# Attention ahead of a mixture of experts: values masked on TensorE, copied by ScalarE, contiguous loads, a later comparison on GpSimd

## The chip, the cores and the metric

The kernel runs on one core of a Trainium2 chip. The metric is the device time of one execution in microseconds (us), as the median of several runs. The profile shows one execution: TensorE appears as PE (matmuls) and PEld (weight loads), VectorE as DVE, ScalarE as ACT, GpSimd as POOL, SyncE as SP, whose queue issues most transfers.

## The reference

```python
def _attn_ref(q, k, v):                    # B, H, S, D = 8, 8, 576, 64
    k_p = k.reshape(B, H, Sp, 8, D).mean(axis=3)      # Sp = 72
    v_p = v.reshape(B, H, Sp, 8, D).mean(axis=3)
    scores = np.matmul(q, k_p.transpose(0, 1, 3, 2)) / np.sqrt(D)
    scores = scores - np.max(scores, axis=-1, keepdims=True)
    attn = np.exp(scores)
    attn = attn / (np.sum(attn, axis=-1, keepdims=True) + 1e-09)
    return np.matmul(attn, v_p)
def reference(...):
    x = attention transposed to (4608, 512)
    x = _moe_ref(x, ...)   # logits = x @ w_gate; greedy choice in order of the logits,
                           # 576 tokens for each of 8 experts; relu(x @ w1[e]) @ w2[e]
    return _moe2_ref(x, ...)   # h = x @ w_in; (h - tanh(h)) @ w_out
```

## The kernel before, in words

The program has three stages: attention over 36 tiles of 128 tokens, the routing and the eight experts, and a dense layer. Each token tile j runs through `scores(j)` and `values(j)`. `scores` multiplies the queries `qT` with the pooled keys `kb` into PSUM (`sc`); VectorE takes the maximum (`mx`) and the difference (`dif`), ScalarE the exponential (`e`). `values` transposes `e` on TensorE (`pt`), ScalarE copies it to SBUF (`et`), TensorE multiplies it with the pooled values (`va`) into the one PSUM tile `av`, and VectorE divides by the sums (`r`, `t`, `x`) and writes the routing logits. A batch element is 576 tokens, so 4.5 tiles: tiles 4, 13, 22 and 31 hold tokens of two batch elements and are multiplied in halves. The last tile writes its product to `sc` instead of `av`.

`pool(b)` sums each eight keys and values of a batch element. For the first element VectorE does it, later GpSimd with six kinds of additions (`pf`, `pg`, then `kb` or `vb`). `rows_of_values(b)` then turns the values: TensorE multiplies `vb` with `turn`, which holds an identity and the gate weights, into 72 columns for each of three row groups; ScalarE copies them to `rows`; VectorE multiplies `rows` with one of two masks in `own` (which of the 96 rows belong to the first head and which to the second) and so fills both halves of `va`.

`first_best(js)` is called after tiles 17, 28, 33 and 35. It makes 32-bit keys of the largest logits: VectorE finds the largest (`m`, `oh`, `mw`, `ohb`), splits the key into `key`, casts it to `hl`, and, for the first two groups, GpSimd compares it with 127 thresholds (`at`, a subtraction and then a comparison with zero).

All of attention is recorded as operations with an urgency, and a planner (`Plan.emit`) writes them into each engine's queue by costs that it estimates. An engine then runs its queue in order. Nearly all instructions have line 123, the recorder's. After attention, routing, experts and the dense layer follow, placed by a plan of their own.

Of the kernel before, what the change touches and what calls it, by code (L numbers as in the profile page):

```python
# [9 lines left out]
F32 = mybir.dt.float32  # L10
# [5 lines left out]
AF = mybir.ActivationFunctionType  # L16
OP = mybir.AluOpType
AX = mybir.AxisListType

B, H, S, D = 8, 8, 576, 64  # L20
SP = S // 8
NP = H // 2
DM = H * D
N = B * S
NT = N // 128
E = 8
# [13 lines left out]

PA, PB1, PD1 = 0.0791790355214496, 0.051241577318574885, 0.039687888533833315
PB2, PD2 = -2.3308446993087815, 2.4448524213730685


class Ring:
# [225 lines left out]
class Kernel:  # L271
# [88 lines left out]
    def attention(self):  # L360
        nc, tc, io, c = self.nc, self.tc, self.io, self.c
        self.L = self.cp.tile([128, NT, 8], F32, name="logits")
        with ExitStack() as st:
            a1 = st.enter_context(tc.tile_pool(name="att1", bufs=1))
            ap = Ring(st.enter_context(tc.tile_pool(name="att", bufs=1)))
            ps = Ring(st.enter_context(tc.tile_pool(name="attp", bufs=1, space=bass.MemoryType.PSUM)), banks=True)
# [7 lines left out]
            half = [slice(0, 64), slice(64, 128)]  # L374


            wg = a1.tile([128, NP, 8], F32, name="wg")
            kb = [a1.tile([128, NP, 2 * SP], F32, name=f"kb{i}") for i in range(2)]
            vb = [a1.tile([128, 2, 3, 96], F32, name=f"vb{i}") for i in range(2)]
            va = [a1.tile([96, 2, 3, 2, 73], F32, name=f"va{i}") for i in range(2)]  # L380
            turn = a1.tile([128, 2, 3, 72], F32, name="turn")
            own = a1.tile([96, 3, 2], F32, name="own")
            junk = a1.tile([128, 512], BF, name="junk")
            nc.vector.memset(junk, 0.0)
            for x in (kb[0], vb[0], kb[1], vb[1]):
                nc.gpsimd.memset(x, 0.0)
            P = self.plan = Plan(nc)
            P.urgency = 900.0
# [1 line left out]

            def turns():
                P.urgency = -2.0
                for h in range(3):
                    for w, r0, r1, hh, pr, _ in parts[h]:
                        eye = c["ident"][half[hh], half[hh]]
                        P.scalar.activation(turn[half[hh], :, h, :64],
                                            eye[:, None, :].to_broadcast([64, 2, 64]), AF.Copy)
                        P.scalar.activation(turn[half[hh], :, h, 64:], wg[half[hh], pr::2], AF.Copy)
                        edge, op = (r1, OP.is_lt) if w == 0 else (r0, OP.is_ge)
                        P.vector.tensor_scalar(own[:, h, w:w + 1], c["pcol"][:96], float(edge), None, op0=op)  # L400
                        for i in range(2):
                            P.vector.tensor_scalar(va[i][:, :, h, w, 72], c["pcol"][:96].to_broadcast([96, 2]),
                                                   float(edge), 8.0, op0=op, op1=OP.mult)

            qT, raw = {}, {}

            def load(b):
                P.urgency = 4.5 * b - 12
                q = qT[b] = ap.tile([128, NP, S], F32, name="qT", bufs=3)
                kr = ap.tile([128, NP, SP, 8], F32, name="kr", bufs=2)  # L410
                vr = ap.tile([128, NP, SP, 8], F32, name="vr", bufs=2)
                raw[b] = kr, vr
                if b == 0:
                    for p in range(NP):
                        P.sync.dma_start(kr[:, p], io["k"][b, :, p])
                    for p in range(NP):
                        P.sync.dma_start(q[:, p, :128], io["q"][b, :, p, :128])
                    for hh in range(2):
                        P.sync.dma_start(wg[half[hh]], io["wg"].rearrange("(p h d) e -> h d p e", h=2, d=64)[hh])
                    for p in range(NP):  # L420
                        P.sync.dma_start(vr[:, p], io["v"][b, :, p])
                    for s0, s1 in ((128, 256), (256, S)):
                        for p in range(NP):
                            P.sync.dma_start(q[:, p, s0:s1], io["q"][b, :, p, s0:s1])
                else:
                    P.sync.dma_start(kr, io["k"][b])
                    P.sync.dma_start(q, io["q"][b])
                    P.sync.dma_start(vr, io["v"][b])
# [39 lines left out]
            def rows_of_values(b):  # L468
                P.urgency = 4.5 * b - 1.3
                for g in range(2):  # L470
                    pt = ps.tile([96, 3, 72], F32, name="pt", bufs=2)
                    for h in range(3):
                        P.tensor.matmul(pt[:, h], vb[b % 2][:, g, h], turn[:, g, h], start=True, stop=True)

                    rows = ap.tile([96, 3, 72], F32, name="rows", bufs=2)
                    P.scalar.activation(rows, pt, AF.Copy)
                    for w in range(2):
                        P.vector.tensor_tensor(va[b % 2][:, g, :, w, :72], rows,
                                               own[:, :, w:w + 1].to_broadcast([96, 3, 72]), op=OP.mult)

            tiles = []
            for j in range(NT):
                pieces, s = [], j * 128
                while s < (j + 1) * 128:
                    b = s // S
                    n = min((b + 1) * S, (j + 1) * 128) - s
# [4 lines left out]
            def scores(j):  # L491

                sc = ps.tile([128, 2, 512], F32, name="sc", bufs=2)
                for pr in range(NP):
                    for b, s0, p0, n in tiles[j]:
                        P.tensor.matmul(sc[p0:p0 + n, pr // 2, (pr % 2) * 144:(pr % 2) * 144 + 144],
                                        qT[b][:, pr, s0:s0 + n], kb[b % 2][:, pr, :], start=True, stop=True)
                sc = sc[:, :, 0:288].rearrange("p a (h s) -> p a h s", h=4)
                mx = ap.tile([128, 2, 4], F32, name="mx", bufs=2)
                P.vector.tensor_reduce(mx, sc, axis=AX.X, op=OP.max)  # L500
                dif = ap.tile([128, 2, 4, SP], F32, name="dif", bufs=2)
                P.vector.tensor_tensor(dif, sc, mx[:, :, :, None].to_broadcast([128, 2, 4, SP]), op=OP.subtract)
                e = ap.tile([128, 6 * 96], F32, name="e", bufs=2)
                P.scalar.activation(e, dif.rearrange("p a h s -> p (a h s)"), AF.Exp, scale=1.0 / 64)
                return e
# [38 lines left out]
            for name, shape, n in (("x", [128, 2, 4, 64], XB), ("t8", [128, 2, 4, 8], 2), ("et", [96, 2, 3, 128], 2),  # L544
                                   ("e", [128, 6 * 96], 2), ("r8", [128, 2, 4], 2)):
                ap.tile(shape, F32, name, n)
            load(0)
            pool(0)
            turns()
            load(1)  # L550
            E1 = {}
            for j in range(NT):
# [73 lines left out]
    def first_best(self, js, pool, engine):  # L626


        c, P = self.c, self.plan
        V = P.vector  # L630
        sg, key = self.best(js, True)
        self.hl = self.rp.tile([128, 2, NT], F32, name="hl")
        self.at7 = pool.tile([128, NT, 127], BF, name="at7")
        at, n = self.at7[:, js], js.stop - js.start
        x = key[:, 0, :, None].to_broadcast([128, n, 127])
        y = c["th7"][:, None, :].to_broadcast([128, n, 127])
        if engine == "vector":
            V.tensor_tensor(at, x, y, op=OP.is_ge)
        else:
            V.tensor_copy(self.hl[:, 0, js], key[:, 0])  # L640
            x = self.hl[:, 0, js, None].to_broadcast([128, n, 127])
            P.gpsimd.tensor_tensor(at, x, y, op=OP.subtract)
            P.gpsimd.tensor_scalar(at, at, 0.0, None, op0=OP.is_ge)
        V.tensor_scalar(sg, sg, 7, -(1 << 31), op0=OP.logical_shift_left, op1=OP.bitwise_xor)
        V.tensor_scalar(key[:, 1], sg, 7, None, op0=OP.arith_shift_right)
        if engine == "vector":
            V.tensor_copy(self.hl[:, :, js], key)
        else:
            V.tensor_copy(self.hl[:, 1, js], key[:, 1])

    def count(self, out, at, js, whole=False):

# [469 lines left out]
    half = [slice(q * HF, (q + 1) * HF) for q in range(2)]  # L1122
# [324 lines left out]
```

## Time and profile before

| what | value |
|---|---|
| time, median of 3 runs | 1525.25 us (1524.16 to 1530.08) |
| the profiled execution, its own time | 1525.06 us |
| its span | 1523.3 us |
| busy in the span: PE, PEld | 95%, 84% |
| busy in the span: DVE, ACT, POOL | 80%, 52%, 20% |
| attention, by the last tile's product | to about 166.7 us |

A share of the span is a mean over stages. Attention is the first ninth of the span; in it no one engine is busy throughout, and the granted clock of TensorE falls in places. The later stages are TensorE work from end to end.

### The profile page before, as it was taken

The page shows a single profiled execution, that of the slowest core. Times are in us where ns is not written, and L with a number is a line of the kernel's source. Part 1 is how long each engine was busy: PE and PEld are TensorE (multiplying, and loading weights), DVE is VectorE, ACT ScalarE, POOL GpSimd, SP SyncE. Part 2 cuts the span into 40 slices and gives each one's busy share as a digit, 9 for nine tenths or more (in the row PEclk, how much of TensorE's full clock was granted, in tenths as well). Part 3 has the DMA queues.
Part 4 walks back from the last instruction along what each step waited for, and adds up shares of the span by engine and source line. Part 5 has one row for each costly group of instructions (what it writes and reads, how often), then busy time and mean ns, then how long its engine had stood idle before and what let it go on. Part 6 is the DMA issues. An engine that isn't in the chain of part 4 may idle for free.

```text
span 1523.3 us, 25631 instructions
## 1 busy us (share of the span) xinstructions
PE 1450.4 (95%) x9764; PEld 1274.2 (84%) x9764; DVE 1218.8 (80%) x2548; ACT 795.7 (52%) x1435; POOL 309.6 (20%) x291
## 2 busy tenths in 40 slices
PE   8989687999999998999999999999999999999997
PEld 6878567999998998999878888888888888888885
DVE  8888777867898888876898788787878788787874
ACT  5334123233554536775666565655656565655653
POOL 4865021101132334553421000010100001010101
PEclk9989788999999999999999999999999999999999
DMA  9951123333342536775201010000101000000000
GB/s 346 352 194 63 43 88 90 101 110 122 128 140 98 168 129 195 261 246 188 93 28 56 1 35 22 28 29 1 56 1 42 14 29 28 23 33 1 28 1 28
DMA packets 100011, 138.51 MB, mean 91 GB/s; under 512 B 7472, under 2 KB 72496, under 8 KB 97200
## 3 DMA queue, kind: packets, MB, share of 16 engines
q1 hardware_dynamic: 89328, 108.04, 21.3%
q0 software_dynamic: 5952, 19.40, 3.7%
q10 hardware_dynamic: 4608, 9.44, 1.6%
q8 instruction: 76, 1.25, 0.3%
q14 instruction: 47, 0.39, 0.1%
HBM read 103.30 MB, written 33.55 MB: 90 GB/s over the span
## 4 chain that ended last, share of the span: by engine, by line
PE 48%; DVE 3%; DMA 1%; issue 1%; ACT 1%; POOL 0%; POOLq 0%; ACTq 0%; SPq 0%; DVEq 0%
PE mm L123 24%; PE m L123 12%; PE rt L123 6%; PE tr L123 6%; DVE g L123 2%; DVE gl L123 1%; DMA wr<-wd 1%; DMA yr<-yd 0%; DVE m L123 0%; ACT parts L123 0%; POOL out L1305 0%; ACT y L123 0%; DVE yl L123 0%; ACT t L123 0%; ACT u L123 0%
## 5 line engine op out<-in xcount | busy, mean ns | idle before, releaser
L123 PE MATMUL mm<-parts 128*128 128x288 f32 x2112 | 308.6, 301 | 3.8 <-DVE parts L123 3.8
L123 PEld LDWEIGHTS mm<-parts 128*128 128x128 f32 x2112 | 289.5, 190 | 7.1 <-DVE parts L123 3.9
L123 PE MATMUL mm<-parts,gh 128*128 128x512 f32 x792 | 244.0, 389 | 0.0
L123 DVE SCALAR_TENSOR_TENSOR g<-s,g 128x512 f32<-128x512 f32 x288 | 205.8, 715 | 2.8
L123 ACT ACTIVATE s<-u,pb 128x512 f32<-128x512 f32 x288 | 192.4, 724 | 0.0
L123 PEld LDWEIGHTS mm<-parts,gh 128*128 128x128 f32 x792 | 148.7, 188 | 30.9
L123 PE MATMUL mm<-parts,gl 128*128 128x512 f32 x396 | 154.5, 390 | 1.6 <-DVE gl L123 1.6
L1305 POOL DMA_INDIRECT out<-y,ix x18 | 19.3, 1072 | 659.6 <-ACT y L123 638.8
L123 PE MATMUL m<-parts 128*128 128x288 f32 x960 | 143.6, 300 | 0.0
L123 PE MATMUL m<-yh,parts 128*128 128x512 f32 x432 | 141.8, 389 | 0.0
L123 ACT ACTIVATE parts<-wr 128x512 fp32r<-128x512 f32 x148 | 90.6, 627 | 82.3 <-PE mm L123 47.4
L123 PEld LDWEIGHTS m<-parts 128*128 128x128 f32 x960 | 131.5, 189 | 2.2 <-issue 1.0
L123 ACT ACTIVATE gh<-g 128x512 fp32r<-128x512 f32 x144 | 91.1, 632 | 76.3 <-DVE g L123 53.8
L123 DVE TENSOR_TENSOR parts<-wr,parts 128x512 fp32r<-128x512 f32 x128 | 100.2, 794 | 30.7 <-ACT parts L123 30.6
L123 DVE TENSOR_TENSOR gl<-g,gh 128x512 fp32r<-128x512 f32 x144 | 105.1, 730 | 21.1 <-ACT gh L123 21.1
L123 DVE COPY_PREDICATED g<-m,t 128x512 f32<-128x512 uint32 x144 | 109.8, 762 | 5.0
L123 ACT ACTIVATE u<-m 128x512 f32<-128x512 f32 x72 | 42.8, 595 | 115.7 <-PE m L123 115.7
L123 PEld LDWEIGHTS m<-yh,parts 128*128 128x128 f32 x432 | 81.1, 188 | 16.9
L123 DVE TENSOR_TENSOR g<-m,u 128x512 f32<-128x512 f32 x72 | 49.5, 687 | 54.2 <-ACT t L123 53.2
L123 PEld LDWEIGHTS mm<-parts,gl 128*128 128x128 f32 x396 | 74.3, 188 | 18.1 <-DVE gl L123 2.9
L123 PE MATMUL m<-yl,parts 128*128 128x512 f32 x216 | 84.1, 389 | 0.0
L123 PE MATMUL tr<-yh,parts 128*128 128x512 f32 x216 | 70.9, 389 | 0.0
(273 smaller groups left out, 2879.7 us busy)
## 6 DMA issues: line engine op xcount, KB each, us to landing
wr<-w SPq DMA_DIRECT2D x64, 512.0 KB, 4.1
xd<-x SPq DMA_DIRECT2D x36, 256.0 KB, 2.1
yd<-y ACTq DMA_DIRECT2D x32, 288.0 KB, 2.3
raw<-wi SPq DMA_DIRECT2D x32, 256.0 KB, 4.3
raw<-wo SPq DMA_DIRECT2D x32, 256.0 KB, 4.2
kr<-k SPq DMA_DIRECT2D x7, 1152.0 KB, 8.3
qT<-q SPq DMA_DIRECT2D x7, 1152.0 KB, 9.8
vr<-v SPq DMA_DIRECT2D x7, 1152.0 KB, 10.4
```

The source lines that it names most:

```text
L123: op = self.call(engine, lambda: f(*args, **kw), ins, outs, cost, delay)
L1305: st = nc.gpsimd.indirect_dma_start(out=self.io["out"], in_=o, in_offset=None, out_offset=bass.IndirectOffsetOnAxis(ap=at, axis=0))
```

## The change

Five edits, all in attention and in `first_best`. First, `turn` gets two halves, one for each mask position, with zeros in the other (a GpSimd memset at the start). The product of `vb` and `turn` is then 144 columns wide and already masked, and one ScalarE copy per group moves it from PSUM straight into `va`; the four VectorE products per batch element and the tile `rows` go. Second, the mask column of `va` is copied from `own` by four VectorE copies, not computed by twelve. Third, the queries lie in HBM so that each part (128, 128 and 320 tokens of the first element) is one contiguous piece per partition: twelve transfers become three, and the gate weights' two become one. Fourth, in `first_best` VectorE makes both key parts and casts them at once before GpSimd's subtraction is recorded. Fifth, `scores` loops over the tile's parts outside and over head pairs inside.

```diff
-            turn = a1.tile([128, 2, 3, 72], F32, name="turn")
+            turn = a1.tile([128, 2, 3, 2, 72], F32, name="turn")
-            for x in (kb[0], vb[0], kb[1], vb[1]):
+            for x in (kb[0], turn, vb[0], kb[1], vb[1]):
                 nc.gpsimd.memset(x, 0.0)
...
+                for hh in range(2):
+                    eye = c["ident"][half[hh], half[hh]]
+                    for h, n in ((0, 2), (1, 1)):
+                        w = hh if n == 2 else 1 - hh
+                        P.scalar.activation(turn[half[hh], :, h::2, w, :64] if n == 2 else turn[half[hh], :, h, w, :64],
...
-                        P.vector.tensor_scalar(own[:, h, w:w + 1], c["pcol"][:96], float(edge), None, op0=op)
-                        for i in range(2):
-                            P.vector.tensor_scalar(va[i][:, :, h, w, 72], c["pcol"][:96].to_broadcast([96, 2]),
-                                                   float(edge), 8.0, op0=op, op1=OP.mult)
+                        P.vector.tensor_scalar(own[:, h, w:w + 1], c["pcol"][:96], float(edge), 8.0, op0=op, op1=OP.mult)
+                for i in range(2):
+                    for g in range(2):
+                        P.vector.tensor_copy(va[i][:, g, :, :, 72], own)
...
-                    for p in range(NP):
-                        P.sync.dma_start(q[:, p, :128], io["q"][b, :, p, :128])
-                    for hh in range(2):
-                        P.sync.dma_start(wg[half[hh]], io["wg"].rearrange("(p h d) e -> h d p e", h=2, d=64)[hh])
+                    P.sync.dma_start(q[:, :NP * 128], io["q"][b, :, :NP * 128])
+                    P.sync.dma_start(wg, io["wg"])
...
-                    pt = ps.tile([96, 3, 72], F32, name="pt", bufs=2)
+                    pt = ps.tile([96, 3, 144], F32, name="pt", bufs=2)
                     for h in range(3):
-                        P.tensor.matmul(pt[:, h], vb[b % 2][:, g, h], turn[:, g, h], start=True, stop=True)
-
-                    rows = ap.tile([96, 3, 72], F32, name="rows", bufs=2)
-                    P.scalar.activation(rows, pt, AF.Copy)
-                    for w in range(2):
-                        P.vector.tensor_tensor(va[b % 2][:, g, :, w, :72], rows,
-                                               own[:, :, w:w + 1].to_broadcast([96, 3, 72]), op=OP.mult)
+                        P.tensor.matmul(pt[:, h], vb[b % 2][:, g, h], turn[:, g, h].rearrange("p w c -> p (w c)"),
+                                        start=True, stop=True)
+                    P.scalar.activation(va[b % 2][:, g, :, :, :72], pt.rearrange("p h (w c) -> p h w c", w=2), AF.Copy)
...
-                for pr in range(NP):
-                    for b, s0, p0, n in tiles[j]:
+                for b, s0, p0, n in tiles[j]:
+                    for pr in range(NP):
...
-        else:
-            V.tensor_copy(self.hl[:, 0, js], key[:, 0])
+        V.tensor_scalar(sg, sg, 7, -(1 << 31), op0=OP.logical_shift_left, op1=OP.bitwise_xor)
+        V.tensor_scalar(key[:, 1], sg, 7, None, op0=OP.arith_shift_right)
+        V.tensor_copy(self.hl[:, :, js], key)
+        if engine == "gpsimd":
             x = self.hl[:, 0, js, None].to_broadcast([128, n, 127])
             P.gpsimd.tensor_tensor(at, x, y, op=OP.subtract)
             P.gpsimd.tensor_scalar(at, at, 0.0, None, op0=OP.is_ge)
```

The planner orders attention anew; behind attention the queues of all engines read as before. Three places matter. The first is VectorE's queue where the second batch element's values are masked (`va_132`), between the divisions of one tile and the next. Before:

```order
L123 TENSOR_TENSOR x_190<-av_167,r_0_198 128x512
L123 TENSOR_REDUCE logits<-t_0_192 128x8
L123 TENSOR_REDUCE mx_219<-sc_217 128x8
L123 TENSOR_TENSOR va_132<-rows_211,own 96x3x72
L123 TENSOR_TENSOR va_132<-rows_212,own 96x3x72
L123 TENSOR_TENSOR va_132<-rows_211,own 96x3x72
L123 TENSOR_TENSOR va_132<-rows_212,own 96x3x72
L123 TENSOR_TENSOR dif_221<-sc_217,mx_219 128x576
L123 TENSOR_REDUCE mx_218<-sc_216 128x8
L123 TENSOR_TENSOR dif_220<-sc_216,mx_218 128x576
```

The same place in VectorE's queue now:

```order
L129 TENSOR_TENSOR x_191<-av_168,r_0_199 128x512
L129 TENSOR_REDUCE logits<-t_0_193 128x8
L129 TENSOR_REDUCE mx_217<-sc_215 128x8
L129 TENSOR_TENSOR dif_219<-sc_215,mx_217 128x576
L129 TENSOR_REDUCE mx_218<-sc_216 128x8
L129 TENSOR_TENSOR dif_220<-sc_216,mx_218 128x576
```

The four products with two operands in SBUF are gone, and the difference follows the maximum at once. The second place is the end of the first group's keys in VectorE's queue (18 logits per partition), among the divisions of tiles 19 and 20. Before:

```order
L123 TENSOR_SCALAR key_225<-sg_224 128x18
L123 RECIPROCAL r_0_198<-r_0_198 128x8
L123 CAST hl_228<-key_225 128x18
L123 TENSOR_TENSOR t_0_192<-av_167,r_0_198 128x64
L123 TENSOR_TENSOR x_188<-av_167,r_0_198 128x512
L123 TENSOR_REDUCE logits<-t_0_192 128x8
L123 TENSOR_SCALAR sg_224<-sg_224 128x18
L123 TENSOR_SCALAR key_225<-sg_224 128x18
L123 TENSOR_REDUCE mx_218<-sc_216 128x8
L123 CAST hl_228<-key_225 128x18
```

And now:

```order
L129 TENSOR_SCALAR key_224<-sg_223 128x18
L129 TENSOR_TENSOR t_0_193<-av_168,r_0_199 128x64
L129 TENSOR_TENSOR x_189<-av_168,r_0_199 128x512
L129 TENSOR_REDUCE logits<-t_0_193 128x8
L129 TENSOR_SCALAR sg_223<-sg_223 128x18
L129 TENSOR_SCALAR key_224<-sg_223 128x18
L129 CAST hl_227<-key_224 128x2x18
```

The one cast of both key parts now stands last; before, the cast that GpSimd's subtraction waits for stood ahead of the second part's shifts. The third place is GpSimd's queue around that subtraction (`at`, 2286 elements). Before:

```order
L123 TENSOR_TENSOR pg_215<-pf_214 128x576
L123 TENSOR_TENSOR pf_214<-vr_205 128x1152
L123 TENSOR_TENSOR at_0_229<-hl_228,th_156 128x2286
L123 TENSOR_TENSOR kb_127<-pg_215 64x4x72 x2
L123 TENSOR_TENSOR pg_215<-pf_214 128x576
L123 TENSOR_TENSOR pf_214<-kr_204 128x1152
```

And now:

```order
L129 TENSOR_TENSOR pg_214<-pf_213 128x576
L129 TENSOR_TENSOR pf_213<-vr_207 128x1152
L129 TENSOR_TENSOR at_0_228<-hl_227,th_157 128x2286
L129 TENSOR_TENSOR kb_128<-pg_214 64x4x72 x2
L129 TENSOR_TENSOR pg_214<-pf_213 128x576
L129 TENSOR_SCALAR at_0_228<-at_0_228 128x2286
```

The subtraction stood ahead of the keys of the seventh batch element (`kb_127`); it now stands ahead of those of the eighth (`kb_128`), so one element's additions later.

## Rows read from the trace of the kernel before

**Rows 1.** Busy time by window: a steady tile, all of attention, the last stage.
```profile
core 0: us, PE busy (x) PEld busy (x) DVE busy (x) ACT busy (x) POOL busy (x), PEclk, DMA share, GB/s
121.10:124.30 3.20, 3.20 (x29) 3.20 (x27) 2.73 (x8) 1.54 (x3) 0.17 (x1) 1.00 0.22 82
12.70:166.70 154.00, 139.70 (x1104) 129.96 (x1104) 132.31 (x332) 63.79 (x138) 88.66 (x84) 0.94 0.58 224
900.00:1523.00 623.00, 612.55 (x2703) 506.90 (x2701) 487.28 (x809) 359.72 (x617) 33.51 (x32) 0.99 0.07 23
```
**Rows 2.** Timeline of PE: products `av` (start, length, [idle before]).
```profile
18.63 1.65 PE L123 MATMUL av<-va,et 96*128 96x146 f32 x12
...
36.66 0.96 PE L123 MATMUL av<-va,et 96*64 96x146 f32 x6
...
44.59 1.70 PE L123 MATMUL av<-va,et 96*128 96x146 f32 x12
...
69.17 1.66 PE L123 MATMUL av<-va,et 96*128 96x146 f32 x12
74.37 2.01 PE L123 MATMUL av<-va,et 96*64 96x146 f32 x24
...
84.22 1.66 PE L123 MATMUL av<-va,et 96*128 96x146 f32 x12
...
88.14 1.70 PE L123 MATMUL av<-va,et 96*128 96x146 f32 x12
94.31 1.82 PE L123 MATMUL av<-va,et 96*128 96x146 f32 x12 [2.75 <-DVE x L123]
...
102.97 1.73 PE L123 MATMUL av<-va,et 96*128 96x146 f32 x12 [0.32 <-DVE x L123]
...
111.48 3.22 PE L123 MATMUL av<-va,et 96*128 96x146 f32 x12
117.57 2.01 PE L123 MATMUL av<-va,et 96*64 96x146 f32 x24
121.19 1.66 PE L123 MATMUL av<-va,et 96*128 96x146 f32 x12
124.32 1.66 PE L123 MATMUL av<-va,et 96*128 96x146 f32 x12
...
165.02 1.76 PE L123 MATMUL sc<-va,et 96*128 96x146 f32 x12 [0.31 <-ACT et L123]
```
**Rows 3.** Timelines around 89 and 103 us: VectorE and GpSimd side by side.
```profile
88.80 4.29 DVE L123 TENSOR_TENSOR va<-rows,own 96x216 f32<-96x216 f32 x4
89.61 2.65 POOL L123 TENSOR_TENSOR pf<-vr 128x1152 f32<-128x1152 f32 x1
...
102.11 4.01 POOL L123 TENSOR_TENSOR at<-hl,th 128x2286 bf16<-128x2286 f32 x1 [9.85 <-DVE hl L123]
102.92 3.23 DVE L123 TENSOR_SCALAR sg<-sg 128x18 int32<-128x18 int32 x1
106.08 1.40 POOL L123 TENSOR_TENSOR kb<-pg 64x288 f32<-64x288 f32 x2
```
**Rows 4.** Groups of attention by form: xcount | busy us, mean ns | idle before.
```profile
L123 ACT ACTIVATE et<-pt 96x384 f32<-96x384 f32 x72 | 32.8, 480 | 35.3 <-PE pt L123 35.0
...
L123 DVE TENSOR_TENSOR va<-rows,own 96x216 f32<-96x216 f32 x32 | 22.8, 756 | 2.1 <-ACT rows L123 2.1
```
**Rows 5.** Timeline of PEld: weight loads of the scores and of the values.
```profile
86.05 1.04 PEld L123 LDWEIGHTS sc<-kb,qT 128*128 128x128 f32 x8
87.02 1.14 PEld L123 LDWEIGHTS pt<-turn,vb 128*96 128x96 f32 x12
```
**Rows 6.** The start: a memset, the first VectorE product, and PE's wait for queries.
```profile
1.12 0.58 POOL L386 MEMSET kb<- 128x576 f32 x1
...
1.20 2.14 DVE L290 TENSOR_SCALAR ident<-jp 128x128 f32<-128x128 f32 x1
...
PE sc L123 <- DMA qT<-q: 3.0, 1, 3.0
```

More of the change, by code (lines that the diff above doesn't have):

```diff
@@ L42, with spans @@
 PB2, PD2 = -2.3308446993087815, 2.4448524213730685
+def spans(b):
+    cuts = sorted({0, S, *(t - b * S for t in range(0, N, 128) if 0 < t - b * S < S)})
+    return list(zip(cuts, cuts[1:]))
 class Ring:
@@ L392, in turns @@
                 P.urgency = -2.0
+                for hh in range(2):
[3 more added lines that the diff above has]
+                        P.scalar.activation(turn[half[hh], :, h::2, w, :64] if n == 2 else turn[half[hh], :, h, w, :64],
+                                            (eye[:, None, None, :] if n == 2 else eye[:, None, :]).to_broadcast(
+                                                [64, 2, 2, 64] if n == 2 else [64, 2, 64]), AF.Copy)
                 for h in range(3):
                     for w, r0, r1, hh, pr, _ in parts[h]:
[L395 to L398, printed above, removed]
+                        P.scalar.activation(turn[half[hh], :, h, w, 64:], wg[half[hh], pr::2], AF.Copy)
                         edge, op = (r1, OP.is_lt) if w == 0 else (r0, OP.is_ge)
-                        P.vector.tensor_scalar(own[:, h, w:w + 1], c["pcol"][:96], float(edge), None, op0=op)
-                        for i in range(2):
-                            P.vector.tensor_scalar(va[i][:, :, h, w, 72], c["pcol"][:96].to_broadcast([96, 2]),
-                                                   float(edge), 8.0, op0=op, op1=OP.mult)
+                        P.vector.tensor_scalar(own[:, h, w:w + 1], c["pcol"][:96], float(edge), 8.0, op0=op, op1=OP.mult)
+                for i in range(2):
+                    for g in range(2):
+                        P.vector.tensor_copy(va[i][:, g, :, :, 72], own)
             qT, raw = {}, {}
@@ L408, in load @@
                 P.urgency = 4.5 * b - 12
-                q = qT[b] = ap.tile([128, NP, S], F32, name="qT", bufs=3)
+                q = qT[b] = ap.tile([128, NP * S], F32, name="qT", bufs=3)
                 kr = ap.tile([128, NP, SP, 8], F32, name="kr", bufs=2)
@@ L422, in load @@
                     for s0, s1 in ((128, 256), (256, S)):
-                        for p in range(NP):
-                            P.sync.dma_start(q[:, p, s0:s1], io["q"][b, :, p, s0:s1])
+                        P.sync.dma_start(q[:, NP * s0:NP * s1], io["q"][b, :, NP * s0:NP * s1])
                 else:
@@ L493, in scores @@
                 sc = ps.tile([128, 2, 512], F32, name="sc", bufs=2)
-                for pr in range(NP):
-                    for b, s0, p0, n in tiles[j]:
+                for b, s0, p0, n in tiles[j]:
+                    for pr in range(NP):
+                        q = qT[b][:, NP * s0 + pr * n:NP * s0 + pr * n + n]
                         P.tensor.matmul(sc[p0:p0 + n, pr // 2, (pr % 2) * 144:(pr % 2) * 144 + 144],
-                                        qT[b][:, pr, s0:s0 + n], kb[b % 2][:, pr, :], start=True, stop=True)
+                                        q, kb[b % 2][:, pr, :], start=True, stop=True)
                 sc = sc[:, :, 0:288].rearrange("p a (h s) -> p a h s", h=4)
@@ L643, in first_best @@
             P.gpsimd.tensor_scalar(at, at, 0.0, None, op0=OP.is_ge)
[L644 to L649, printed above, removed]
     def count(self, out, at, js, whole=False):
@@ L1427, in heads, with queries @@
         return np.ascontiguousarray(x).reshape(B, 128, NP, *tail)
+    def queries(x):
+        x = heads(x, S)
+        to = np.empty((B, 128, NP * S), x.dtype)
+        for b in range(B):
+            for s0, s1 in spans(b):
+                to[b, :, NP * s0:NP * s1] = x[b, :, :, s0:s1].reshape(128, -1)
+        return to
     arrays = {
-        "q": heads(q, S),
+        "q": queries(q),
         "k": heads(k, SP, 8),
         "v": heads(v, SP, 8),
-        "wg": np.ascontiguousarray(moe_w_gate),
+        "wg": np.ascontiguousarray(np.asarray(moe_w_gate).reshape(NP, 128, E).transpose(1, 0, 2)),
         "w1": np.ascontiguousarray(moe_w1),
```

## The prediction

> **What bounds the kernel now.** I read the busy time by window first. In the last stage TensorE works 612.55 of 623.00 us [rows 1], so whatever attention ends earlier or later should arrive at the end of the program undiminished: nothing behind it has room to absorb or to add. Attention is another matter: in 154 us no engine is full, and the granted clock averages 0.94 [rows 1]. So the question is what tile after tile costs there, and which tiles cost more.
>
> The products `av` are one per tile, so their starts in TensorE's timeline are the kernel's metronome. From 121.19 to 124.32 it is 3.13 us [rows 2], and in that window TensorE's weight loads are busy all 3.20 us while VectorE is busy 2.73 [rows 1]: an undisturbed tile is TensorE's. A tile that carries a batch element's values costs 3.92 (84.22 to 88.14), 0.79 more, and a tile in halves 3.62 (117.57 to 121.19), 0.49 more [rows 2]. From tile 5 (44.59) to tile 35 (165.02), 120.4 us pass [rows 2]. Thirty plain tiles are 93.9, six elements' values 4.7, three split tiles 1.5: 100.1. So 20.3 us there are disturbance, and the row-to-row gaps show where: 69.17 to 74.37 is 2.1 above a plain tile, 88.14 to 102.97 (three tiles) 5.4 above, 102.97 to 117.57 (two tiles and an element's values, 7.05) 7.6 above [rows 2]; the other 5.2 lie in places whose rows are not shown. From tile 0 (18.63) to tile 5, 26.0 us pass for five tiles, one element and one split tile, 16.9: 9.0 more of it, of which 4.3 between tile 4 (36.66) and tile 5 [rows 2].
>
> Then I laid VectorE and GpSimd side by side at these gaps. At 88.80 four masking products take 4.29 us together, while GpSimd runs its sum `pf` of 2.65 us; at 102.92 a shift of 18 integers per partition takes 3.23 us, until GpSimd's subtraction, which began at 102.11 and takes 4.01, is over [rows 3]. Over attention the 32 masking products take 22.8 us, 756 ns each [rows 4]. VectorE's work with all operands in SBUF thus waits for GpSimd's instructions, and the wait reaches TensorE: at 94.31 it has stood idle for 2.75 us for VectorE's `x`, which frees the one PSUM tile [rows 2]. A second cost comes behind such a gap: the product at 111.48 takes 3.22 us where the next full one takes 1.66 [rows 2], which is the ratio of the clock's two levels, 1.2 and 2.4 GHz.
>
> **The change part by part.** *Masking moves to TensorE and ScalarE.* It removes all 32 VectorE products, so 22.8 us of VectorE's time [rows 4]. That is not the gain by itself; the gain is the disturbance above plain tiles that these waits make. In exchange TensorE multiplies 144 columns, not 72. I price that by the scores, whose products are 144 columns wide: eight weight loads in 1.04 us, 0.130 each, against twelve in 1.14, 0.095 each [rows 5]. Twelve at 0.130 are 1.56, so +0.42 us per element; at the least nothing, if the loads alone set the pace, and at most a doubling, +1.14. I take 0.45, as the values' instructions come in one run with nothing between them. ScalarE copies 432 elements per partition instead of 216; by the copy of 384 in 480 ns [rows 4] that is about 0.54 us, twice per element, and ScalarE is busy 1.54 of 3.20 us in a steady tile [rows 1]. It costs nothing there; without that cover it would be some 0.4 us per element. The chain from product to `va` even gets shorter by a VectorE step.
>
> *Start.* GpSimd's memset of `turn` has 864 elements per partition; at 0.58 us for 576 [rows 6] it takes 0.87. VectorE's first product `ident` was held for 2.14 us until the memsets were over [rows 6], so the whole start of VectorE's queue moves back by 0.9; the eight mask instructions saved are too short to give that back. The twelve query transfers that become three, and gate weights in one, free SP's queue; TensorE waited 3.0 us for queries once [rows 6], and all loads behind come sooner. But tile 0 hangs on VectorE's sums of the first keys and values, not on queries, so I give half of that 3.0 as a gain: bounds 0 and 3.0. With the 4.3 us before tile 5, which are a masking wait, tile 5 comes 4.3 + 1.5 − 0.9 = 4.9, say 5.0 us earlier, at 39.6. Bounds: 2.5 (half of the stall is replaced by a wait for the second element's values, which GpSimd can only sum once they have landed) and 8.0 (nearly all of the 9.0).
>
> *The keys.* The shifts now stand ahead of the subtraction, so they no longer wait for its 4.01 us [rows 3]; GpSimd gets the subtraction an element later. What else changes is less friendly. Before, GpSimd stood idle 9.85 us for the cast [rows 3], so the other key instructions found it quiet; now it is at its sums while VectorE makes keys. Nine of the eleven key instructions of the first group have only SBUF operands. Counting in tiles: the sums of the sixth element begin just ahead of tile 15's product, run some eleven us (two of 2.65, 1.40 for the keys [rows 3], and the other three kinds at as much again less 1, an estimate), and the keys begin behind tile 17's logits, about as late, so I expect the first six to find GpSimd quiet, and the last three (shift, shift, cast, behind tile 19's logits) to meet the seventh element's keys `kb`, 1.40 us in two instructions [rows 3], of which I charge 1.5. The instructions' own time is mostly hidden by VectorE's 0.47 us of room per tile [rows 1]; I charge 1.2 for the first group and 0.3 for the second. Together 3.0; bounds 0 (all in quiet) and 8.0 (each of the nine waits, half of them for a 2.65-us sum with room taken off).
>
> Here a rule speaks against the change. The Trainium skill, page "SBUF — State Buffer", section "Who interferes with whom", says that a VectorE instruction with two SBUF inputs, and `copy`, `cast` and `tensor_scalar` in their two-port modes, share a port pair with GpSimd, and that the one that issues second blocks for the other's whole instruction; one with a single SBUF input outside these modes does not. The trace agrees in the 3.23-us shift and the 4.29-us products [rows 3]. By the rule the key instructions left on VectorE are exposed to any sum that GpSimd is at, which is the first rival below; by the rows alone only the three last are.
>
> *The loop order in `scores`* changes four tiles' order of halves only: the second element's keys are wanted later in them. I cost it at nothing; at worst a split tile's 0.49 doubles, at best it goes.
>
> *The sum.* From tile 5 at 39.6: 93.9 + 6 × (0.79 + 0.45) + 1.5 + 3.0 = 105.8, so tile 35 at 145.4, not 165.02: 19.6 us earlier. From there on every queue reads as before, so the profiled execution's 1525.06 becomes 1505.5. Its time lies 0.2 us below the median of the runs, 1525.25, so I forecast **1505.5 us**. A change of 0.5% (7.6 us) is about the least that a measurement of this kernel can tell from none.
>
> **The rivals.** *The waits return at the keys.* GpSimd, no longer idle for the cast, is at its sums at tiles 18 to 20, and nine key instructions wait for it, also once in the second group. Keys cost 8 and the start gives only 2.5: tile 35 at 152.9, 1513. For it: the shift in rows 3 shows what one such wait costs. Against it: my count gives GpSimd a rest just there, since the next keys `kb` must wait for TensorE's scores.
>
> *More goes than I count.* If the first five tiles lose 8.0 and the keys cost nothing, tile 35 comes at 36.6 + 93.9 + 7.4 + 1.5 = 139.4, so 1499.5; and with the wider values at no cost, 1497. For it: the clock fell only behind gaps, and the gaps go. Against it: VectorE must still sum two elements' keys in these tiles.
>
> *The masking waits did not set the pace.* If TensorE would have waited anyway, for GpSimd's sums themselves, the same 20.3 us return as waits for `kb` or `va`, and 6 × 0.45 + 0.9 us are added: 1528.7, no change. For it: GpSimd is busy 88.66 of 154 us [rows 1], so its sums could be late somewhere. Against it: in the steady window it is busy 0.17 of 3.20 us and the tiles are no faster [rows 1].
>
> *Slower.* The gain is lost to the clock. If the new order leaves TensorE a gap of about the 2.75 us at 94.31, and the clock then stays at the lower level, a product takes 3.22 instead of 1.66 [rows 2], and a tile some 3.0 us more. Ten such tiles beyond those of before eat the 19.6 and add 10: 1535. From seven tiles on the gain is gone, from ten on the kernel is slower by over 0.5%; the rows show one product so slow, and the next at full clock.
>
> **How the numbers follow.** My forecast, within about 4 us, has a chance of 0.60; more gain (below 1501) 0.15; waits at the keys (1510 to 1517) 0.15; no pace set by the masking 0.06; slower 0.04. The range of **1497 to 1516** reaches over the first three and leaves out the last two and the far ends of the others, about 2 in 10. Faster by over 0.5% (below 1517.6) has 0.89, as a little of the key rival lies above that; within 0.5% 0.07; slower by more 0.04.
>
> **What would show it.** Right: tile 5's product near 39.6 and tile 35's near 145 us; no VectorE instruction of over 1.5 us between them, save perhaps one shift or cast near tile 20; twelve values' weight loads at about 1.5 us; granted clock of attention near 0.98; busy times behind attention as before. Wrong: a plain tile that is no longer 3.13 us; a wait of TensorE for ScalarE's `va` or for GpSimd's `vb`; key instructions of 2 us and more; or a later stage that takes another time than before, which would break the step from attention's end to the program's.

## The result and the profile after

The changed kernel takes **1508.74 us** (median of 4 runs, 1507.44 to 1510.01) against 1527.35 in the runs of before taken beside it (4 runs, 1524.16 to 1530.08): ratio 0.9872, 95% interval 0.9854 to 0.9889. The forecast was 1505.5, range 1497 to 1516. The profiled execution took 1509.08 us, its span 1507.3; against the profiled execution of before that is 16.0 us.

Busy time by window, with the columns of [rows 1]:

```profile
12.70:150.00 137.30, 134.96 (x1103) 128.68 (x1102) 106.72 (x297) 65.20 (x138) 87.50 (x84) 0.99 0.62 244
885.00:1507.00 622.00, 611.59 (x2699) 506.08 (x2697) 486.43 (x808) 359.58 (x616) 34.49 (x32) 1.00 0.07 23
```

TensorE is busy nearly throughout attention now (134.96 of 137.30 us) at a granted clock of 0.99, and VectorE has lost some 25 us of work and waiting in it. The last stage is as before [rows 1]. The timeline of PE shows the metronome, the products `av`, at the places that answer to [rows 2]:

```profile
18.68 1.66 PE L129 MATMUL av<-va,et 96*128 96x146 f32 x12
...
36.29 2.01 PE L129 MATMUL av<-va,et 96*64 96x146 f32 x24
39.88 1.66 PE L129 MATMUL av<-va,et 96*128 96x146 f32 x12
...
99.03 1.66 PE L129 MATMUL av<-va,et 96*128 96x146 f32 x12
102.62 1.98 PE L129 MATMUL av<-va,et 96*64 96x146 f32 x24
106.21 1.67 PE L129 MATMUL av<-va,et 96*128 96x146 f32 x12
109.36 1.72 PE L129 MATMUL av<-va,et 96*128 96x146 f32 x12
112.55 1.70 PE L129 MATMUL av<-va,et 96*128 96x146 f32 x12
117.19 1.66 PE L129 MATMUL av<-va,et 96*128 96x146 f32 x12
...
148.63 1.76 PE L129 MATMUL sc<-va,et 96*128 96x146 f32 x12 [0.31 <-ACT et L129]
```

Tile 5 (39.88) comes 4.7 us earlier, tile 35 (148.63) 16.4 us earlier than in [rows 2]. A plain tile still takes 3.11 to 3.19 us (109.36 to 112.55 is 3.19), a tile with an element's values 4.64 (112.55 to 117.19), and a tile in halves 3.59 on each side. No product takes 3.22 us any more. What became of [rows 3] stands in the timelines of VectorE and GpSimd:

```profile
93.75 0.16 DVE L129 TENSOR_SCALAR sg<-sg 128x18 int32<-128x18 int32 x1
93.89 1.44 POOL L129 TENSOR_TENSOR kb<-pg 64x288 f32<-64x288 f32 x2 [6.46 <-PE sc L129]
93.95 0.64 DVE L129 TENSOR_SCALAR key<-sg 128x18 int32<-128x18 int32 x1
94.62 0.18 DVE L129 CAST hl<-key 128x36 f32<-128x36 int32 x1
```

The shift that took 3.23 us takes 0.16. The next one takes 0.64 because GpSimd's `kb` has just begun, which is the one wait at the keys that the forecast charged, at a third of its price.

### The profile page after: what moved, and what is told of

It reads as the page before. It is cut to its first block, busy times and chain, and to the rows that moved or that the text cites. A ratio compares the mean times of both kernels' runs of the same rounds, so it can differ in the third digit from the quotient of the medians.

```text
span 1507.3 us, 25587 instructions
## 1 busy us (share of the span) xinstructions
PE 1445.5 (96%) x9763; PEld 1272.5 (84%) x9764; DVE 1194.8 (79%) x2506; ACT 796.2 (53%) x1433; POOL 311.5 (21%) x292
## 4 chain that ended last, share of the span: by engine, by line
PE 77%; DVE 16%; DMA 3%; issue 2%; ACT 1%; POOL 1%; SPq 0%; POOLq 0%; ACTq 0%; DVEq 0%
PE mm L129 36%; PE m L129 17%; PE tr L129 7%; PE rt L129 7%; PE av L129 4%; DVE parts L129 3%; PE sc L129 3%; PE pt L129 2%; DVE g L129 2%; DVE ca L129 2%; PE rt L659 1%; DVE oa L129 1%; DVE at L129 1%; DVE ob L129 1%; DMA wr<-w 1%
```

## The experiments

The theory: VectorE's masking products with both operands in SBUF waited for GpSimd's sums, and TensorE waited for them, also at half clock behind the gaps. The rivals: the loads carry the gain; the keys carry it; VectorE's work as such was the cost, not its waiting. In each run the planner orders attention anew, so what an edit gives includes what its new order gives.

The half clock can be read in the kernel before, in the longest wait of TensorE and behind it (columns of [rows 1]); the granted clock of 0.50 is the lower level, 1.2 GHz:

```profile
106.00:109.50 3.50, 0.34 (x3) 0.13 (x3) 3.38 (x10) 1.18 (x3) 3.27 (x5) 1.00 0.46 195
109.50:114.50 5.00, 4.97 (x25) 4.96 (x25) 3.13 (x7) 1.63 (x4) 4.58 (x8) 0.50 0.15 56
```

**The masking edit alone**, on the kernel before:

```diff
-                    pt = ps.tile([96, 3, 72], F32, name="pt", bufs=2)
+                    pt = ps.tile([96, 3, 144], F32, name="pt", bufs=2)
-                    rows = ap.tile([96, 3, 72], F32, name="rows", bufs=2)
...
+                    P.scalar.activation(va[b % 2][:, g, :, :, :72], pt.rearrange("p h (w c) -> p h w c", w=2), AF.Copy)
```

> The kernel before with the masking edit alone (the turn tile in two halves, the 144-column product, ScalarE's copy straight into va, the mask column by four copies); loads, key order and loop order stay as before. Theory (the gain of the whole change, 18.6 us, is the masking products' waits for GpSimd and the half clock behind the gaps): 13 to 17 us faster than before, tile 35's product at 149 to 152 us, a shift of about 3 us of the first keys still there since GpSimd's subtraction still stands ahead of it. Rival 'keys': the masking is worth 10 us or less and a gap at the first keys remains with a slow product behind it. Rival 'loads': 10 us or less, tile 5 comes at 42 us or later.

Measured: 1512.01 us, ratio 0.9890 (0.9866 to 0.9915), so 1.10 of the 1.28 per cent. Tile 5 comes at 42.09, tile 35 at 151.14. Two long waits are left on VectorE, both at the keys, one in each group; VectorE and GpSimd in the timeline:

```profile
94.55 4.01 POOL L123 TENSOR_TENSOR at<-hl,th 128x2286 bf16<-128x2286 f32 x1 [6.22 <-DVE sg L123]
94.58 4.01 DVE L123 TENSOR_SCALAR key<-sg 128x18 int32<-128x18 int32 x1
98.52 1.40 POOL L123 TENSOR_TENSOR kb<-pg 64x288 f32<-64x288 f32 x2
...
130.61 2.38 DVE L123 TENSOR_SCALAR key<-sg 128x11 int32<-128x11 int32 x1
```

A shift of 18 numbers per partition issued 0.03 us after GpSimd's subtraction lasts exactly as long as that. This is as the theory had it; the gain, 17.4 us, lies a little above its 13 to 17.

**The loads alone** (`queries()`, three query transfers, one for the gate weights):

```diff
-                    for p in range(NP):
-                        P.sync.dma_start(q[:, p, :128], io["q"][b, :, p, :128])
+                    P.sync.dma_start(q[:, :NP * 128], io["q"][b, :, :NP * 128])
```

> The kernel before with the load edit alone (each part of the queries one contiguous piece per partition, nine transfers fewer for the queries, one for the gate weights); nothing else. Theory: within 1.5 us of before; tile 4's product 0.2 to 0.4 us earlier than 36.66, tile 5 still behind the stall, near 44.3. Rival 'loads': 4 us faster or more, tile 5 before 41 us.

Measured: 1527.12 us, ratio 0.9983 (0.9966 to 1.0). The second element's values land much sooner, so that GpSimd's first sum starts at 21.63 us (before 26.08), but the time does not show it; GpSimd, VectorE and TensorE in the timeline:

```profile
21.63 2.64 POOL L129 TENSOR_TENSOR pf<-vr 128x1152 f32<-128x1152 f32 x1 [16.68 <-DMA vr<-v]
...
41.25 6.05 DVE L129 TENSOR_TENSOR va<-rows,own 96x216 f32<-96x216 f32 x4
...
46.59 3.00 PE L129 MATMUL av<-va,et 96*64 96x146 f32 x18 [3.31 <-DVE va L129]
51.48 1.66 PE L129 MATMUL av<-va,et 96*128 96x146 f32 x12
```

The stall for the masked values, here inside tile 4 (46.59), is still there, and longer than in the kernel before: in this execution, the longest of its 12 runs, tile 5 comes at 51.48, not near 44.3 as expected. The median lies 2.3 us below that of before, and the theory had 1.5 at most; but the rival wanted 4 us or more and tile 5 before 41, so the rival that the loads carry the gain falls.

**The keys alone** (both shifts and one cast ahead of GpSimd's subtraction):

```diff
-            V.tensor_copy(self.hl[:, 0, js], key[:, 0])
+        V.tensor_copy(self.hl[:, :, js], key)
+        if engine == "gpsimd":
```

> The kernel before with the order of the keys alone (both shifts and one cast ahead of GpSimd's subtraction); the masking products stay on VectorE. Theory: 0 to 4 us faster: the 3.23-us shift goes, but the masking products still wait for GpSimd's sums. Rival 'keys': 6 us faster or more, with the gap of 102.97 to 117.57 us gone. A third outcome, slower: GpSimd's subtraction now lands on the masking products of the seventh element, which then wait 4 us: 0 to 4 us slower.

Measured: 1526.5 us, ratio 0.9982 (0.9967 to 0.9997): some 3 us, inside the theory's 0 to 4 and short of the rival's 6. The 3.23-us shift is gone, and with it the gap that the rival named: from tile 20 to tile 22 it takes 8.22 us (105.99 to 114.21) instead of 14.60 (102.97 to 117.57). But the masking products wait longer elsewhere; the group of 12.7 to 150 us:

```profile
L123 DVE TENSOR_TENSOR va<-rows,own 96x216 f32<-96x216 f32 x32 | 27.2, 894 | 0.8 <-ACT rows L123 0.6
```

**The same products on VectorE, but from PSUM.** This tells waiting from working:

```diff
-                    rows = ap.tile([96, 3, 72], F32, name="rows", bufs=2)
-                    P.scalar.activation(rows, pt, AF.Copy)
-                        P.vector.tensor_tensor(va[b % 2][:, g, :, w, :72], rows,
+                        P.vector.tensor_tensor(va[b % 2][:, g, :, w, :72], pt,
```

> The kernel before, but the four masking products per element read TensorE's result in PSUM instead of ScalarE's copy in SBUF, so that one operand alone is in SBUF; the copy 'rows' is gone; VectorE's products, their count and their elements stay as before. Theory 'two SBUF operands wait': the products take 0.3 to 0.4 us each (22.8 us in all becomes 10 to 13), none is held while GpSimd sums, the stalls at tiles 5, 15 and 19 go and the time falls by 9 to 15 us, most of what the whole change gives. Rival 'VectorE's work as such': VectorE still does the 32 products on the path, so less than 6 us.

Measured: 1515.89 us, ratio 0.9921 (0.9899 to 0.9943). The group of these products, and VectorE beside GpSimd at the second element's:

```profile
L123 DVE TENSOR_TENSOR va<-pt,own 96x216 f32<-96x216 f32 x32 | 10.7, 370 | 1.0 <-PE pt L123 0.9
...
35.94 2.64 POOL L123 TENSOR_TENSOR pf<-vr 128x1152 f32<-128x1152 f32 x1
36.07 0.62 DVE L123 TENSOR_TENSOR va<-pt,own 96x216 f32<-96x216 f32 x2
36.73 0.37 DVE L123 TENSOR_TENSOR va<-pt,own 96x216 f32<-96x216 f32 x1
```

Thirty-two products of the same size on the same engine take 370 ns each and not 756 [rows 4], and three run to their end inside GpSimd's sum. So VectorE's work was no cost; the second SBUF operand was. (This kernel also lacks ScalarE's copy to `rows`; what that alone gives was not run.) The Trainium skill, "SBUF — State Buffer", section "Who interferes with whom", says the same: with two SBUF inputs a VectorE instruction contends with a GpSimd instruction that reads SBUF, and with at most one, outside the two-port modes, it does not. The trace agrees on both sides, with 756 and 370 ns. What this kernel doesn't win of the whole gain shows in one chain, as in the kernel before: GpSimd's subtraction holds the shift, the exponential `e` and the copy `et` come late behind it, TensorE waits 2.84 us for `et`, and the product behind the wait runs at half clock:

```profile
92.00 4.01 POOL L123 TENSOR_TENSOR at<-hl,th 128x2286 bf16<-128x2286 f32 x1 [5.84 <-DVE hl L123]
92.81 3.23 DVE L123 TENSOR_SCALAR sg<-sg 128x18 int32<-128x18 int32 x1
97.59 0.68 ACT L123 ACTIVATE e<-dif 128x576 f32<-128x576 f32 x1 [6.39 <-DVE dif L123]
98.79 2.16 PE L123 MATMUL pt<-turn,vb 128*96 128x72 f32 x12 [2.84 <-ACT et L123]
100.75 3.22 PE L123 MATMUL av<-va,et 96*128 96x146 f32 x12
```

**The change without its masking edit**, and the same **with the keys as before too**:

```diff
-                    pt = ps.tile([96, 3, 144], F32, name="pt", bufs=2)
+                    pt = ps.tile([96, 3, 72], F32, name="pt", bufs=2)
...
+                        P.vector.tensor_tensor(va[b % 2][:, g, :, w, :72], rows,
```

> The changed kernel with the masking put back on VectorE (72 columns, the copy 'rows', four products per element with two SBUF operands); loads, key order and loop order as changed. Theory: most of the gain is lost, 1521 to 1526 us (13 to 17 above the changed kernel, 1508.7), with the masking products again at 20 us and more in all and single groups of 2 us and more beside GpSimd's sums. Rival 'the loads and keys carry the gain': below 1516 us.

> The changed kernel with the masking back on VectorE and the order of the keys as before too, so that loads and loop order alone are left of the change. With the new order of the keys that kernel took 1530.2 us, against 1527 before, although loads alone and keys alone gave 1527.1 and 1526.5. If the moved subtraction of GpSimd makes the masking products wait more: 1524 to 1527.5 us. If the earlier loads bring GpSimd's sums onto the masking products and the keys do nothing: 1529 to 1532 us.

Measured: 1530.18 us, ratio 1.0021 (1.0005 to 1.0036), and 1531.33, ratio 1.0013 (0.9994 to 1.0032). Both lie above the 1521 to 1526 of the first expectation: with the masking left on VectorE the rest of the change is worth nothing, though loads alone and keys alone had each seemed to give 2 to 3 us. The second run, inside the second of its two ranges, doesn't blame the keys, since undoing them changes nothing. It differs from the loads alone in the loop order only, and yet lies 4 us above them. The group of the first kernel (12.7 to 166 us), and a tile in it:

```profile
L129 DVE TENSOR_TENSOR va<-rows,own 96x216 f32<-96x216 f32 x32 | 25.9, 851 | 1.1 <-ACT rows L129 0.9
...
152.48 3.70 PE L129 MATMUL av<-va,et 96*64 96x146 f32 x24 [2.47 <-DVE x L129]
```

The waits are again at 25.9 us, and the product behind a wait of 2.47 us takes 3.70 us where the changed kernel's takes 1.98 to 2.01. Why small edits add up so badly here is not settled. One observation bears on it: kernels with these products repeat poorly, 1522.4 to 1535.6 us in 23 runs of before and 1523.5 to 1537.6 in 12 of the second kernel here, while the changed one stays within 2.6 us in 4, and its six variants further below within 4 us in 5 to 8 runs each. The kernel of before that masks from PSUM lies between, 7.1 us in 6 runs. Differences of 2 or 3 us between kernels with these products say little.

**The changed kernel with VectorE masking from PSUM** (72 columns again):

> The changed kernel, but TensorE writes 72 columns again and VectorE masks them from PSUM (four products per element, one SBUF operand each); no 'rows', no GpSimd memset of turn. Theory 'two SBUF operands wait, and the wider product costs some 0.5 to 0.75 us per element': the products take 0.33 to 0.40 us each, none waits, TensorE saves 0.42 us and more per element and the start 0.8: 1503 to 1508 us. Rival 'VectorE's work on the path': VectorE's 1.4 us more per element delay the maxima and the divisions, 1510 to 1518 us.

Measured: 1507.32 us, ratio 0.9868 (0.9852 to 0.9885), not to be told from the change. The products take 373 ns, 10.6 us in all, and no cost of them shows; tile 35 comes 2.4 us earlier (146.27). Where attention has room on VectorE, TensorE need not do the masking.

**The values' product twice:**

```diff
+                        for _ in range(2):
-                        P.tensor.matmul(pt[:, h], vb[b % 2][:, g, h], turn[:, g, h].rearrange("p w c -> p (w c)"),
+                            P.tensor.matmul(pt[:, h], vb[b % 2][:, g, h], turn[:, g, h].rearrange("p w c -> p (w c)"),
```

> The changed kernel, but each values' product of vb and turn is done twice into the same PSUM tile (the result is the same; the work added is twelve weight loads, about 1.47 us, for each of the eight elements). Theory 'an element's values stand on TensorE's path with their whole length': 1.4 to 1.6 us more for each of seven elements behind the first, 9 to 13 us slower than the changed kernel, 1518 to 1522 us. Rival 'TensorE waits anyway where the values stand, so the width costs only in part': less than 6 us slower.

Measured: 1522.56 us, 13.8 above the changed kernel, a little beyond the 9 to 13 expected. In the profiles tile 0 comes 2.65 us later (21.33 against 18.68), which the expectation left out, and from tile 5 to tile 35 it takes 118.63 us instead of 108.75, 9.9 more for six elements. The weight loads of the values, one row of each kernel, first the changed one, then this one, then the 72 columns from PSUM:

```profile
115.60 1.51 PEld L129 LDWEIGHTS pt<-turn,vb 128*96 128x96 f32 x12
```
```profile
125.43 2.98 PEld L129 LDWEIGHTS pt<-turn,vb 128*96 128x96 f32 x24
```
```profile
114.45 1.09 PEld L129 LDWEIGHTS pt<-turn,vb 128*96 128x96 f32 x12 [0.32 <-issue]
```

These rows belong to the seventh element. The step of its tile is 4.64, 6.11 (122.38 to 128.49) and 4.25 us (111.28 to 115.53), so 1.51, 2.98 and 1.12 above a plain tile. Up to 0.03 us this element costs the whole length of its weight loads: nothing hides it. For the six elements together the added loads, six times 1.47, are 8.8 of the 9.9 us.

**The scores' loop order as before:**

```diff
-                for b, s0, p0, n in tiles[j]:
-                    for pr in range(NP):
+                for pr in range(NP):
+                    for b, s0, p0, n in tiles[j]:
```

> The changed kernel with the loop order of the scores as before (head pairs outside, parts inside); all else as changed. Theory: within 1.5 us of the changed kernel, the steps into and out of the tiles in halves stay at 3.5 to 3.7 us each. Rival 'the order by parts costs': the step into a tile in halves falls to 3.2, 1.5 us in all. Rival 'the order by parts gains': a wait of TensorE for the second element's keys returns in front of these tiles, 2 us or more slower.

Measured: 1509.38 us, ratio 0.9883 (0.9868 to 0.9899), the same time, but tile 35 at 147.27, 1.4 us earlier; from tile 5 (40.05) on it is 1.5 us. The steps that hold the scores of a tile in halves are 0.24 to 0.52 us shorter; the steps on each side of its `av` stay at 3.59. So the rival's 1.5 us is there in attention, though not at the step that it named, and it doesn't show in the time. PE in front of the last such tile, in the changed kernel and in this one:

```profile
128.59 1.19 PE L129 MATMUL sc<-kb,qT 128*64 128x144 f32 x8
```
```profile
127.71 0.71 PE L129 MATMUL sc<-kb,qT 128*64 128x144 f32 x8
```

**The second element's keys on GpSimd**, and **the zero fills on ScalarE**:

```diff
-                    if b == 0 or (b == 1 and nm == "k"):
+                    if b == 0:
```
```diff
-                nc.gpsimd.memset(x, 0.0)
+                nc.scalar.activation(flat, junk[:, :1].to_broadcast([128, flat.shape[1]]), AF.Copy)
```

> The changed kernel, but the keys of the second batch element are summed by GpSimd instead of VectorE (a condition in the pooling). In the changed kernel tiles 0 to 3 take 12.2 us where three plain tiles take 9.4, while VectorE sums these keys in four reductions of 0.74 us and GpSimd stands idle for 16.7 us. Theory 'VectorE is what the first tiles wait for once the masking is off it': 1 to 3 us faster than the changed kernel. Rival 'GpSimd's sums come one behind the other, so the values of the second element are late': tile 4 and tile 5 come 2 us and more later, 1 to 4 us slower.

> The changed kernel, but the five zero fills at the start (kb, turn, vb) are done by ScalarE as copies of a zero column, not by GpSimd. VectorE's first product, ident, is held for 2.91 us there until GpSimd's fills are over, and the first sum of keys starts at 6.16. Theory 'that hold, with the 0.82 us of the wider turn in it, sets the start': ident takes under 0.5 us, the first sum starts before 5 us, tile 0's product is 1 to 2.5 us earlier and the time 0.5 to 2.5 us shorter. Rival 'the transfers set the start': the first sum starts sooner but the tiles from 2 on stay where they are, within 0.5 us of the changed kernel.

Measured: 1509.86 us, ratio 0.9880 (0.9854 to 0.9906), and 1509.13, ratio 0.9868 (0.9843 to 0.9894): neither is told from the changed kernel. With the keys on GpSimd tiles 0 to 3 take 11.5 us instead of 12.2, but tile 0 and tile 5 come 1.1 us later each (19.74 and 41.02): neither theory's size came. The zero fills did what was expected of them in the start; VectorE in the changed kernel and in this one:

```profile
1.20 2.91 DVE L296 TENSOR_SCALAR ident<-jp 128x128 f32<-128x128 f32 x1
...
6.16 0.73 DVE L129 TENSOR_REDUCE k<-kr 128x72 f32<-128x576 f32 x1
```
```profile
1.20 0.26 DVE L296 TENSOR_SCALAR ident<-jp 128x128 f32<-128x128 f32 x1
...
3.63 0.75 DVE L129 TENSOR_REDUCE k<-kr 128x72 f32<-128x576 f32 x1 [0.26 <-DMA kr<-k]
```

The hold is gone, and the first sum starts 2.5 us sooner. Tile 0 comes 1.23 us sooner (17.45 against 18.68), tile 35 1.21 us sooner (147.42): the start's gain goes through attention undiminished. In this execution the stretch behind tile 35 was 1.4 us longer than in that of the changed kernel (1360.1 against 1358.7), so the span doesn't show it. Of the 0.5 to 2.5 us expected in the time nothing is seen, and the runs can't tell so little.

**The three edits that helped attention, together:** VectorE from PSUM, zero fills on ScalarE, loop order as before.

> The changed kernel with three edits that were each run alone: VectorE masks from PSUM and TensorE's product is 72 columns wide (alone: tile 35 at 146.27 against 148.63 us, 1507.3 us), the zero fills on ScalarE (alone: tile 35 at 147.42, 1509.1 us), the scores' loop order as before (alone: tile 35 at 147.27, 1509.4 us). If the three gains in attention add up, tile 35 comes at 143.4 to 145 us and the time is 1503 to 1505.5 us, so faster than the changed kernel by 0.2 to 0.4%. Rival 'they hide in one another': tile 35 at 146 us or later, 1506 to 1509 us.

Measured: 1506.35 us (5 runs, 1504.83 to 1508.65), ratio 0.9862 (0.9843 to 0.9880). In attention the gains add up almost fully: tile 35 at 144.29, 4.3 us earlier than in the changed kernel, of 4.9 summed. That is inside the theory's 143.4 to 145. The profiled span is 4.2 us shorter (1503.1 against 1507.3), but the median only 2.4: it lies above the 1503 to 1505.5 expected and among the rival's times. Its median is the lowest of this study, but its interval overlaps that of the change.

## Why the prediction was right, and what was off

The mechanism was right, and so were the direction and the range; the time came out 3.2 us above the forecast (of the profiled executions, 16.0 us gained where 19.6 were forecast). Point by point:

- **The masking waits set the pace: shown for the larger part.** Alone the edit gives 17.4 us; the rest of the change without it gives none; the same products with one operand in PSUM give 13.5. The rival that the masking did not set the pace, at 1528.7, fell with this. But the largest gap of before, the 14.60 us from tile 20 to tile 22, is the held shift's: with masking from PSUM these two steps still take 13.83 us (92.77 to 106.60), with the keys reordered 8.22. The masking edit alone brings them to 10.35 (94.36 to 104.71) though its shift is held for 4.01; TensorE has scores and the values' product to do meanwhile. So some 4 of its 17.4 us come from the planner's new order, an estimate from these steps.
- **Tile 5, forecast 39.6, measured 39.88.** The sum held, but partly by luck: two errors in it cancel. The start was to gain 0.6 us (1.5 for the loads less 0.9 for the memset), and tile 0 comes at 18.68 where before it came at 18.63. From tile 0 to tile 5 it takes 21.20 us instead of 25.96, so 4.8 less, where 4.3 were forecast for the stall. The memset was right in size (0.82 us, and `ident` held for 2.91 instead of 2.14). The 1.5 for the loads is not shown: the wait for queries is still there, 2.04 us once. Beside the masking edit alone the changed kernel has tile 0 1.55 us earlier and tile 5 2.2 us (18.68 and 39.88 against 20.23 and 42.09), so most of the difference lies ahead of tile 0. There the queries land 0.36 us sooner, TensorE has 14 instead of 20 instructions of scores between that wait and the product, and its granted clock is higher (0.63 from 12.35 to 15.5 us, against 0.50 from 12.71 to 16.2). No run separates the loads from the new order. With the loads alone tile 0 came 1.0 us later than before (19.63), at a granted clock of 0.51 from 15.0 to 19.6. TensorE's wait for queries and tile 0 with the masking edit alone, then the wait in the changed kernel:

```profile
12.71 2.29 PE L123 MATMUL sc<-kb,qT 128*128 128x144 f32 x8 [2.40 <-DMA qT<-q]
20.23 1.66 PE L123 MATMUL av<-va,et 96*128 96x146 f32 x12
```
```profile
12.35 0.51 PE L129 MATMUL sc<-kb,qT 128*128 128x144 f32 x2 [2.04 <-DMA qT<-q]
```

- **From tile 5 to tile 35, forecast 105.8, measured 108.75.** This is where the 3 us are lost. An element's values, read at the seventh, cost 1.51 and not 1.24: the wider product was sized well (+0.37 by the weight loads, forecast 0.45), but the base of 0.79, read in one window of before, was too small. The step read there, 84.22 to 88.14, holds all of the values' weight loads, but only four of a tile's six transposes of `e`; the other two stand in the next step, which was disturbed anyway. PEld of before, a plain step and this one:

```profile
82.46 0.47 PEld L123 LDWEIGHTS pt<-ident,e 128*96 128x96 f32 x4
83.89 0.25 PEld L123 LDWEIGHTS pt<-ident,e 128*96 128x96 f32 x2
...
85.59 0.47 PEld L123 LDWEIGHTS pt<-ident,e 128*96 128x96 f32 x4
87.02 1.14 PEld L123 LDWEIGHTS pt<-turn,vb 128*96 128x96 f32 x12
```

  Six elements at this price are 9.1, not 7.4: +1.6. A tile in halves costs 0.46 on both sides, and one side was read: 2.8 for three, not 1.5: +1.3. The loop order, costed at nothing, is 1.5. What remains for the keys and all else is 1.5, not 3.0: −1.5. Together 2.9; the keys, charged too high, hide a third of what the other three lack.
- **The waits at the keys** (the rival at 1513) did not return: the longest key instruction takes 0.64 us. With the masking edit alone, where the subtraction stands ahead of the shift, that took 4.01.
- **The slower rival** needed a wait of about 2.75 us of TensorE between the tiles; there is none, and the granted clock is 0.99.
- **Attention's gain arrives at the end:** of 16.4 us at tile 35, 16.0 are in the profiled time.

## What to carry to other kernels

Price an engine's instructions by what they wait for, not by what they do: taking the masking off VectorE was worth 17 us of 1527 chiefly because its second SBUF operand made it wait for GpSimd, and reading the operand from PSUM gives most of that with an edit of three lines. When TensorE becomes the bound, read each added product at the full length of its weight loads, and see that the step you read holds all of a tile's other instructions. An edit that feeds a stalled chain sooner, like the loads here, may show its worth only after the stall is gone; no run here tells, so it would have to be run alone there too.

## What the runs showed of the hardware that was not expected

- Four products of scores show as eight matmul instructions. With 64 tokens the eight take 0.71 us when the products go in turn to the two halves of the PSUM partitions, and 1.19 us when all four go to one half (0.089 against 0.149 us an instruction); with all 128 tokens eight take 1.15 us in the changed kernel. Two halves in turn thus seem to overlap in TensorE; that they do is inferred from these times, not shown apart.
- A VectorE product over 128 columns (`ident`) was held through five GpSimd memsets in a row, 2.91 us, and took 0.26 us without them: it did not get in between two of them. At the keys the 0.64-us shift did: it ended with the first of two `kb` additions, and the cast behind it took 0.18 us.
